# Gated attention into a routed expert layer on one core: fewer blocks in the DMA transposes, a z that is copied across, and a ring of row pairs

## The chip, the cores and the metric

One core of one Trainium2 chip. The metric is the device time of one execution in microseconds (us). TensorE (PE) multiplies, ScalarE (ACT) and VectorE (DVE) work element by element, GpSimd (POOL) issues the indirect transfers and all transfers that change the type, and SyncE (SP) issues the others; all transfers run on the same 16 DMA engines.

## The reference

```
B, S, D = 8, 2816, 256                      # u, v: (B, S, D) float32; z: (B, S, 64)
scores = z @ z.T / S                        # per batch
out    = u * (relu(scores)**2 @ v)
x      = out.reshape(22528, 256)
dense  = relu(x @ w1_dense) @ w2_dense      # 256 -> 512 -> 256
e, p   = argmax and softmax of x @ w_gate   # 8 experts
result = dense + p[e] * (relu(x @ w1[e]) @ w2[e])
```

## The kernel before

The program has two parts that meet in DRAM. The **attention part** goes through the 8 sequences (batches) in order. A sequence is 22 blocks of 128 tokens; blocks are numbered g = 0 to 175 over all sequences, and the program calls `tick(g)` once for each, about half-way and at the end of each pair of blocks; `at` and `soon` hang work on a tick by its number. The scores of a group of 2 or 4 query blocks against pairs of key blocks are made from zT, the transposed z, with two matmuls side by side on 64 rows of the array each (L408). For that, zT holds the 64 features of a block twice, on partitions 0 to 63 and 64 to 127. ScalarE and VectorE make relu and square (L423, L425, L436, L438) into a tile A. Since the scores are symmetric, part of A is not computed but transposed by DMA from an earlier group's A (L493), inside the tile of the later group or into the memory of the weights `wall`, which are loaded later. The product with v is L610, and it takes two finished blocks at a time.

`load_z` brings the next sequence's z in with GpSimd's queue. `turn_z`, called twice for a sequence at the border between two sequences, lets VectorE double 11 blocks of it (L115), and SP transposes the doubled copy, 11 blocks of 128 x 128 at a time (L118).

When two blocks are finished, `gate_x` multiplies them by u into `pays` (L637), a ring of 22 rows of 384 values, of which 256 are data, 4 hold the gate's value and the token's number and the rest is padding. SP transposes the pair for the router (L639): from the start of one row to the end of the data of the next, that is 5 blocks of 128 columns, of which 4 are data. `routing(q)` handles 11 blocks at once (fewer at the end, `sizes`), 5 ticks after the last of them: logits, the expert of each token, and its place in the list of its expert. `route_b` writes gate and token into the rows of `pays`, and `scatter(g)` casts the places of one block (L777) and has GpSimd write its 128 rows of 576 bytes to `xs` in DRAM (L779). One block is sent each tick (`one_scatter`, first come first served), two while rows 143 to 153 are waiting, each of these followed by a small copy on GpSimd (`paced`).

The **expert part** begins with rows 0 to 153, whose table of tiles (`table(0)`) is known by then; `fetch` (from tick 170 on, SP) reads 256 tokens of one expert transposed from `xs` (L954) with gates and tokens (L956). A `slot` is one such tile: `up` (L1003), relu on ScalarE (L1006), `down` for both experts (L1012), the sum (L1029, L1030), and the indirect write of the result by GpSimd (L1032), with a small copy (`pause`, L1017) behind the first half. The rows that are not yet sent go out between the slots: four at slot 0, two at slot 1, then one at each slot s with s % 6 == 4, each with a pause behind it. All must be gone before slot 61, from which on tiles need the second table. GpSimd's instructions run in the order in which the program gives them (`behind`).

The order of PE, ACT, DVE and SP is made while the program is built: `offer` hands out the work of ScalarE and VectorE by a model of the time (`now`, `free`), and each instruction waits in its engine's queue in that order.

Of the kernel before, what the change touches and what calls it, by code (L numbers as in the profile page):

```python
# [8 lines left out]
F32 = mybir.dt.float32  # L9
# [6 lines left out]
P = 128  # L16
# [3 lines left out]
def kernel(  # L20
# [34 lines left out]
    ROW = 288  # L55
    WIDE = 384
    CAP = N
# [43 lines left out]
    ecap = const.tile([P, E], F32, name="ecap")  # L101
    pays = const.tile([P, 2 * G, WIDE], BF, name="pays")

# [4 lines left out]

    def turn_z(b, k0, k1):

        if k0 == 0:
            assert not any(left[m] for m in left if groups[m][0] == b - 2)
            zn_of[b] = zpool.tile([P, nK, 2, dq], BF, name="zn", bufs=1)
            zT_of[b] = zpool.tile([P, nK, P], BF, name="zT")
# [7 lines left out]
        if k1 == nK:  # L122
            z_there.add(b)
# [17 lines left out]

    z_of, zn_of, zT_of, v_of, ut_of, xT_of, lg_of, rs = {}, {}, {}, {}, {}, {}, {}, {}

# [249 lines left out]
    def scores(n, ks, x=None):  # L393

        open_group(n)
        b, i0, w = groups[n]
        zT = zT_of[b]
        c = w * P
        while n == 0 and z0_left and parts0[z0_left[0]][0] <= ks[-1] + (4 if ks[0] else 1):
# [12 lines left out]
        relu(n, ks, s, c, now[0] + 0.2, sx)  # L412
        run(now[0] + (0.4 if n + ks[0] == 0 else 0.0))
# [59 lines left out]
    def block(n, k, c):  # L473

        w = groups[n][2]
        for a in far[n]:
            _, j0, wj = groups[a]
            if j0 <= k < j0 + wj:
                x = c * wj + k - j0
                return turned_to(a, n, w)[:, x * P:(x + 1) * P]  # L480
        return A[n][:, k, c * P:(c + 1) * P]

# [150 lines left out]
    def gate_x(g, o):  # L633
        g0 = g % (2 * G)
        x = pays[:, g0:g0 + 2, 0:D]
        assert g + 1 < 2 * G or (g - 2 * G in placed and g + 1 - 2 * G in placed)
        nc.vector.tensor_mul(x, o[:, :, 0:D], ut_of.pop(g))  # L637
        xT = aw.tile([P, 5, P], BF, name="xT", bufs=8)
        nc.sync.dma_start_transpose(  # L639
            out=xT[:], in_=pays[:, g0:g0 + 2, :].rearrange("p n r -> p (n r)")[:, 0:5 * P])  # L640
        issue(1.25)
        for j in range(2):
            xT_of[g + j] = xT[:, 3 * j:3 * j + 2, :]

# [62 lines left out]
    def route_b(q):  # L707
# [5 lines left out]
        def one():  # L713
            se = vec("se", n)
            nc.vector.tensor_reduce(out=se, in_=ex, axis=AX.X, op=ALU.add)
            o = starts[q] % (2 * G)
            rows = pays[:, o:o + n, :]
# [19 lines left out]
        def three():  # L737
            nc.vector.tensor_add(inc, inc, pre[1])
            nc.vector.tensor_mul(inc, inc, oh)
            pos = vec("pos", n, bufs=5)  # L740
            nc.vector.tensor_reduce(out=pos, in_=inc.rearrange("p e t -> p t e"),
                                    axis=AX.X, op=ALU.add)
            rs[q] = pos

# [23 lines left out]
    def paced(g):  # L768
        scatter(g)
        behind(lambda: nc.gpsimd.tensor_copy(rest[:], pays[:, g % (2 * G), 0:160]))  # L770

    def scatter(g):
        q = max(q for q in range(nQ) if starts[q] <= g)
        j = g - starts[q]

        pi = rt.tile([P, 1], I32, name="pi", bufs=16)
        nc.vector.tensor_copy(pi[:], rs[q][:, j:j + 1])  # L777
        free["pool"] = max(free["pool"], now[0]) + 1.5
        ins = behind(lambda: nc.gpsimd.indirect_dma_start(  # L779
            out=xs, out_offset=bass.IndirectOffsetOnAxis(ap=pi[:], axis=0),  # L780
            in_=pays[:, g % (2 * G), 0:ROW].bitcast(F32), in_offset=None))
        if q < Q1:
# [343 lines left out]
    placed = set()  # L1126

    def one_scatter(dve=True):
        if not waiting:
            return  # L1130
        g = waiting.pop(0)
        if dve:
            send = paced if (Q1 - 1) * G <= g < Q1 * G else scatter
            offer(now[0], 0, {"dve": (0.1, lambda eng: send(g))}, lambda t: placed.add(g))
        else:
            scatter(g)
            placed.add(g)

    routed = []
# [58 lines left out]
    def first_fetch(s):  # L1198
        assert not waiting or waiting[0] >= Q1 * G
        got[s] = fetch(s)  # L1200
# [7 lines left out]

    def tick(g):
        for fn in later.pop(g, []):  # L1210
            fn()
        one_scatter()
        if waiting and (Q1 - 1) * G <= waiting[0] < Q1 * G:
            one_scatter()
# [15 lines left out]
    late["y"] = pool("psY", 2, space=bass.MemoryType.PSUM)  # L1230
    for s in range(NT - MAYBE + 2):
        assert s + AHEAD < NT1 or not waiting, (s, len(waiting))
        slot(s, NT - MAYBE)
        for fn in later.pop(nB + s, []):
            fn()
        for _ in range(4 if s == 0 else 2 if s == 1 else s % 6 == 4):
            if waiting:
                g = waiting[0]
                one_scatter(dve=False)
                pause(pays[:, g % (2 * G), 0:ROW].bitcast(F32))  # L1240
    assert not waiting
# [39 lines left out]
```

## Time and profile before

| | us |
|---|---|
| median of 3 runs (905.73 to 906.49) | 906.41 |
| the profiled execution, its own time | 910.9 |
| its span, first to last instruction | 909.2 |
| TensorE busy in the span | 865.5 |
| VectorE, ScalarE, GpSimd busy | 669.7, 702.9, 486.0 |
| mean granted clock of TensorE | 0.992 of 2.4 GHz |

The rows below come from the one profiled execution, which took 4.5 us more than the median. Busy time of an engine that does not set the end says little; the views by stretch and the chain of waits tell which one does.

### The profile page before, as it was taken

What the parts mean: (1) busy time and instruction counts of PE and PEld (TensorE: products, weight loads), DVE (VectorE), ACT (ScalarE), POOL (GpSimd) and SP (SyncE); (2) the same over time, 40 slices, a digit from 0 to 9 for tenths busy, and PEclk for the clock granted to TensorE, in tenths of its full rate; (3) what the DMA queues carried; (4) which work ended last, traced back from release to release, by engine and by line L of the source; (5) the groups of instructions that cost most, each with busy time, mean ns of one, the idle gap of its engine ahead of it and who ended that gap; (6) DMA issues with size and microseconds to landing.
All of it is one profiled execution on the core that took longest, in us unless ns stands there. A gap on an engine that the chain in (4) does not pass through costs nothing.

```text
span 909.2 us, 30147 instructions
## 1 busy us (share of the span) xinstructions
PE 865.5 (95%) x12178; PEld 757.4 (83%) x12178; DVE 669.7 (74%) x1275; ACT 702.9 (77%) x873; POOL 486.0 (53%) x538
## 2 busy tenths in 40 slices
PE   7999897999999999999999999899999999999996
PEld 5898796898898898788898878688887888888885
DVE  8989695898997998897998985545654444546663
ACT  8989695897897897797897984566766776777664
POOL 7202343244344344344244374778787887777765
PEclk9999999999999999999999999999999999999999
DMA  8998999999999999999999867555544544544333
GB/s 175 174 199 152 179 175 133 172 196 199 194 190 174 200 177 163 192 204 180 200 170 179 148 143 135 118 123 113 113 113 108 115 111 115 112 102 102 92 94 86
DMA packets 289246, 136.80 MB, mean 150 GB/s; under 512 B 258638, under 2 KB 266062, under 8 KB 289104
## 3 DMA queue, kind: packets, MB, share of 16 engines
q1 hardware_dynamic: 263552, 79.40, 52.4%
q0 software_dynamic: 25552, 55.44, 27.4%
q8 instruction: 96, 1.57, 0.7%
q14 instruction: 46, 0.38, 0.1%
HBM read 61.54 MB, written 37.03 MB: 108 GB/s over the span
## 4 chain that ended last, share of the span: by engine, by line
PE 62%; POOL 15%; issue 12%; DVE 5%; DMA 3%; ACT 2%; POOLq 0%; another core or an unknown queue 0%; DVEq 0%; ACTq 0%
PE o L610 41%; POOL out_dram L1032 11%; PE s L408 9%; PE yy L1012 5%; PE h_ps L1003 5%; POOL zr L1017 3%; DMA wall<-A 1%; DVE r L425 1%; PE lg L671 1%; DMA vb<-in_v_dram 1%; ACT A L436 1%; DVE pays L637 1%; DVE ring L1030 1%; DVE A L438 1%; ACT r L423 1%
## 5 line engine op out<-in xcount | busy, mean ns | idle before, releaser
L610 PE MATMUL o<-vb,A 64*128 64x256 bf16 x7184 | 464.4, 270 | 8.5 <-issue 5.8
L610 PEld LDWEIGHTS <-A 64*128 64x128 bf16 x7184 | 381.5, 94 | 51.3 <-issue 10.7
L779 POOL DMA_INDIRECT xs<-pays,pi x176 | 189.1, 1075 | 281.2 <-DVE pi L777 232.5
L423 ACT ACTIVATE r<-s 128x1024 f32<-128x1024 f32 (+1 forms) x246 | 242.5, 1010 | 50.3 <-PE s L408 48.0
L436 ACT ACTIVATE A<-r 128x1024 bf16<-128x1024 f32 (+1 forms) x246 | 248.7, 1042 | 8.7 <-issue 3.1
L1006 ACT ACTIVATE ring<-h_ps 128x1024 bf16<-128x1024 f32 x180 | 184.6, 1026 | 90.8 <-PE h_ps L1003 51.7
L425 DVE TENSOR_SCALAR r<-s 128x1024 f32<-128x1024 f32 x151 | 182.8, 1219 | 14.3 <-PE s L408 12.4
L1030 DVE SCALAR_TENSOR_TENSOR ring<-yy,me,ring 128x256 f32<-128x256 f32 x179 | 86.3, 482 | 141.4 <-ACT ring L1029 70.9
L438 DVE TENSOR_TENSOR A<-r 128x1024 bf16<-128x1024 f32 x145 | 175.3, 1218 | 3.8 <-ACT r L423 2.8
L1032 POOL DMA_INDIRECT out_dram<-ring,me x140 | 145.5, 1039 | 54.9 <-DVE ring L1030 27.2
L1012 PEld LDWEIGHTS <-ring 128*128 128x128 bf16 x1432 | 139.3, 98 | 34.9 <-issue 17.1
L408 PE MATMUL s<-zT 64*128 64x512 bf16 (+1 forms) x874 | 146.9, 357 | 7.7 <-ACT r L423 2.4
L1012 PE MATMUL yy<-w2d,ring 128*128 128x256 bf16 x716 | 107.8, 273 | 12.2 <-DVE ring L1030 11.6
L1012 PE MATMUL yy<-ring 128*128 128x256 bf16 x716 | 107.9, 273 | 2.4 <-ACT ring L1006 1.4
L1003 PE MATMUL h_ps<-ring,w1d 128*128 128x256 bf16 x720 | 93.7, 274 | 2.6 <-ACT ring L1006 2.6
L1003 PE MATMUL h_ps<-ring 128*128 128x256 bf16 (+1 forms) x872 | 93.5, 253 | 0.6 <-ACT ring L1006 0.6
L990 DVE COPY ring<-wall 128x2048 bf16 x109 | 82.9, 775 | 11.6 <-issue 7.1
L637 DVE TENSOR_TENSOR pays<-o,ut 128x512 bf16<-128x512 f32 x88 | 60.2, 684 | 38.7 <-PE o L610 16.9
L1029 ACT COPY ring<-yy 128x256 f32<-128x256 f32 x179 | 67.3, 376 | 23.2 <-PE yy L1012 11.4
L1003 PEld LDWEIGHTS <-ring 128*128 128x128 bf16 x872 | 73.5, 98 | 8.5 <-issue 1.2
L1003 PEld LDWEIGHTS <-w1d 128*128 128x128 bf16 x720 | 70.2, 98 | 11.2 <-issue 2.9
L408 PEld LDWEIGHTS <-zT 64*128 64x128 bf16 x874 | 54.7, 94 | 23.9 <-issue 11.2
(124 smaller groups left out, 448.2 us busy)
## 6 DMA issues: line engine op xcount, KB each, us to landing
ut<-in_u_dram SPq DMA_DIRECT2D x88, 256.0 KB
vb<-in_v_dram POOLq DMA_DIRECT2D x14, 704.0 KB
wall<-in_moe_w_dram POOLq DMA_DIRECT2D x16, 256.0 KB
xs<-pays,pi POOLq DMA_INDIRECT x176
zr<-in_z_dram POOLq DMA_DIRECT2D x7, 352.0 KB
out_dram<-ring,me POOLq DMA_INDIRECT x140
ring<-xs SPq DMA_TRANSPOSE x114
xT<-pays SPq DMA_TRANSPOSE x88
```

Of the source, the lines that this page charges most:

```text
L408: nc.tensor.matmul(out=s[:, h, y * c:(y + 1) * c], lhsT=zT[r, k + h, :], rhs=zT[r, i0:i0 + w, :], start=True, stop=True)
L423: nc.scalar.activation(r[:, :, :c], s[:, :, :c], AF.Relu, scale=1.0 / S)
L425: nc.vector.tensor_scalar(out=r[:, :, :c], in0=s[:, :, :c], scalar1=1.0 / S, scalar2=0.0, op0=ALU.mult, op1=ALU.max)
L436: nc.scalar.activation(a, r, AF.Square)
L438: (nc.gpsimd if eng == "pool" else nc.vector).tensor_mul(a, r, r)
L610: nc.tensor.matmul(out=o[:, j, 0:D], lhsT=block(n, k, i + j - i0)[r], rhs=v_of[b][r, k, :], start=(p == 0 and x == 0), stop=(p == 1 and x ...
L779: ins = behind(lambda: nc.gpsimd.indirect_dma_start(out=xs, out_offset=bass.IndirectOffsetOnAxis(ap=pi[:], axis=0), in_=pays[:, g % (2 * G ...
L1003: nc.tensor.matmul(out=h_ps[:, f, hs, :], lhsT=w1(c, f), rhs=xT[:, hs, c, :], start=(c == 0), stop=(c == 1))
L1006: nc.scalar.activation(h[:, :, 0:m * P], h_ps[:, :, 0:m, :].rearrange("p f h t -> p f (h t)"), AF.Relu)
L1012: nc.tensor.matmul(out=y[:, k, :], lhsT=h[:, f, j * P:(j + 1) * P], rhs=w2(f), start=(f == 0), stop=(f == 3))
L1030: nc.vector.scalar_tensor_tensor(out=ys, in0=y[:, 1, :], scalar=me[:, j, 0:1], in1=yd, op0=ALU.mult, op1=ALU.add)
L1032: ins = behind(lambda: nc.gpsimd.indirect_dma_start(out=out, out_offset=bass.IndirectOffsetOnAxis(ap=ids[j], axis=0), in_=ys, in_offset=No ...
```

## The change

The transposed part of a finished pair is now exactly its data: `pays` holds 16 pairs of 544 values, in which the second row's data follow the first row's at once, so 4 blocks are transposed instead of 5. The first row's gate and token now lie on the first 4 values of the second row; so these are written only when the row is sent (L777's place; the cast of the places is made once for each routing), and the first row of a pair may go only 4 ticks after the second (3 for rows 143 to 153). `next_row` picks the next one: a first row whose partner left long enough ago, else a second row. z is transposed as it is loaded, two blocks of 64 features in one of 128 columns, so in 11 blocks and one transfer; every second column block of zT is filled. VectorE then copies the two halves across the partitions (`cross_z`), at ticks 9 and 11 of the sequence before. Where the halves of a block pair now stand in the other order, the indices of A follow (`block`). Late rows go out at every fifth slot.

```diff
+    WIDE = 2 * D + ROW - D
+    PAIRS = 16
+    pays = const.tile([P, PAIRS, WIDE], BF, name="pays")
+    def row(g):
+        return pays[:, g // 2 % PAIRS, g % 2 * D:g % 2 * D + ROW]
-    def turn_z(b, k0, k1):
-        nc.vector.tensor_copy(
-            zn_of[b][:, k0:k1, :, :],
-            z_of[b][:, k0:k1, :].unsqueeze(2).to_broadcast([P, k1 - k0, 2, dq]))
+    def turn_z(b):
+        assert not any(left[m] for m in left if groups[m][0] == b - 2)
+        zT_of[b] = zpool.tile([P, nK, P], BF, name="zT")
         nc.sync.dma_start_transpose(
-            out=zT_of[b][:, k0:k1, :],
-            in_=zn_of[b][:, k0:k1].rearrange("p k h d -> p (k h d)"))
+            out=zT_of[b].rearrange("p (j e) c -> p j e c", e=2)[:, :, 0, :],
+            in_=z_of[b][:].rearrange("p k d -> p (k d)"))
+    def cross_z(b, h):
+        zT = zT_of[b].rearrange("p (j e) c -> p j e c", e=2)
+        r, o = (slice(x * dq, (x + 1) * dq) for x in (h, 1 - h))
+        nc.vector.tensor_copy(zT[r, :, 1, :], zT[o, :, 0, :])
+        if h == 1:
             z_there.add(b)
...
-    nc.vector.memset(pays[:, :, D:], 0.0)
+    nc.vector.memset(pays[:, :5, :], 0.0)
+    nc.vector.memset(pays[:, 5:, 2 * D:], 0.0)
...
-                nc.tensor.matmul(out=s[:, h, y * c:(y + 1) * c], lhsT=zT[r, k + h, :],
+                nc.tensor.matmul(out=s[:, h, y * c:(y + 1) * c], lhsT=zT[r, k + h * own, :],
...
-        xT = aw.tile([P, 5, P], BF, name="xT", bufs=8)
-        nc.sync.dma_start_transpose(
-            out=xT[:], in_=pays[:, g0:g0 + 2, :].rearrange("p n r -> p (n r)")[:, 0:5 * P])
+        xT = aw.tile([P, 4, P], BF, name="xT", bufs=8)
+        nc.sync.dma_start_transpose(out=xT[:], in_=x)
...
-            nc.vector.reciprocal(rows.bitcast(F32)[:, :, P], se)
-            nc.vector.tensor_copy(rows.bitcast(I32)[:, :, P + 1], tok[:, starts[q]:starts[q + 1]])
+            gt = gt_of[q] = rt.tile([P, G, 2], F32, name="gt", bufs=5)
+            nc.vector.reciprocal(gt[:, :n, 0], se)
+            nc.vector.tensor_copy(gt[:, :n, 1].bitcast(I32), tok[:, starts[q]:starts[q + 1]])
...
+            pi = rt.tile([P, G], I32, name="pi", bufs=5)
+            nc.vector.tensor_copy(pi[:, :n], pos)
...
-        pi = rt.tile([P, 1], I32, name="pi", bufs=16)
-        nc.vector.tensor_copy(pi[:], rs[q][:, j:j + 1])
+        nc.vector.tensor_copy(row(g)[:, D:D + 4].bitcast(F32), gt_of[q][:, j, :])
...
-            soon(t - 1 if b else 5, lambda b=b: turn_z(b + 1, 0, nK // 2), 0.4)
-            soon(t if b else 6, lambda b=b: turn_z(b + 1, nK // 2, nK), 0.4)
+            at(t - 1 if b else 5, lambda b=b: turn_z(b + 1))
+            for h in range(2):
+                soon(t + 9 + 2 * h, lambda b=b, h=h: cross_z(b + 1, h), 0.8)
...
+    def next_row():
+        even = [g for g in waiting if g % 2 == 0 and
+                sent.get(g + 1, 9e9) <= clock[0] - (3 if (Q1 - 1) * G <= g < Q1 * G else 4)]
+        odd = [g for g in waiting if g % 2]
+        return (even or odd or [None])[0]
...
-        for _ in range(4 if s == 0 else 2 if s == 1 else s % 6 == 4):
+        for _ in range(4 if s == 0 else 2 if s == 1 else s % 5 == 4):
```

## Rows read from the trace of the kernel before

**Rows 1.** The page of the profile, its parts 1 and 2: busy time of the engines over the whole execution; then the 40 slices of the span, of TensorE and the DMA engines, in tenths.

```profile
...
PE 865.5 (95%) x12178; PEld 757.4 (83%) x12178; DVE 669.7 (74%) x1275; ACT 702.9 (77%) x873; POOL 486.0 (53%) x538
...
PE   7999897999999999999999999899999999999996
...
DMA  8998999999999999999999867555544544544333
...
```

**Rows 2.** The page, its part 3: the queue of SP (packets, megabytes, share of the 16 engines' span), and the view of DMA issues: the two transposes that the change touches.

```profile
...
q1 hardware_dynamic: 263552, 79.40, 52.4%
...
xT<-pays SPq DMA_TRANSPOSE x88
...
zT<-zn SPq DMA_TRANSPOSE x14
...
```

**Rows 3.** Busy time of each engine by stretch of 5 us, with the granted clock, the share of the 16 DMA engines and the rate, before and in two halts of TensorE.

```profile
...
75.00:80.00 5.00, 5.00 (x87) 4.54 (x85) 4.92 (x9) 5.00 (x6) 2.75 (x3) 1.00 0.43 92
...
85.00:90.00 5.00, 5.00 (x90) 4.73 (x88) 5.00 (x7) 5.00 (x6) 1.94 (x2) 1.00 1.16 199
...
95.00:100.00 5.00, 4.91 (x94) 4.15 (x90) 1.73 (x7) 1.53 (x3) 1.94 (x2) 1.00 1.10 201
...
105.00:110.00 5.00, 4.73 (x48) 3.05 (x49) 3.37 (x12) 3.94 (x5) 0.97 (x1) 0.66 1.06 222
145.00:150.00 5.00, 4.52 (x77) 4.03 (x73) 4.97 (x10) 4.76 (x6) 2.77 (x4) 1.00 1.01 61
150.00:155.00 5.00, 0.84 (x10) 0.68 (x12) 0.97 (x2) 0.56 (x1) 1.72 (x2) 0.94 1.16 186
...
```

**Rows 4.** The chain of work that ended last, 80 to 112 us (start, length, what).

```profile
...
95.45 7.64 DMA wall<-A
...
103.25 1.06 ACT A L436
...
```

**Rows 5.** Who waited for whom, 90 to 110 us (us in total, times, longest).

```profile
...
ACT A L436 <- DMA wall<-A: 3.0, 1, 3.0
...
PE s L408 <- ACT r L423: 2.4, 1, 2.4
...
```

**Rows 6.** What SP's queue issued, 76 to 104 us (start, time that the issue took).

```profile
...
83.25 1.81 SPq L639 DMA_TRANSPOSE xT<-pays  x1
...
86.50 3.72 SPq L118 DMA_TRANSPOSE zT<-zn  x2
...
91.46 2.25 SPq L493 DMA_TRANSPOSE wall<-A  x1
94.14 1.21 SPq L639 DMA_TRANSPOSE xT<-pays  x1
95.45 2.22 SPq L493 DMA_TRANSPOSE wall<-A  x1
...
```

**Rows 7.** Who waited for whom on SP's queue, the whole span: the z transposes.

```profile
...
SPq L118 <- DVE pi L777: 8.5, 6, 2.2
...
SPq L118 <- DVE A L438: 5.1, 2, 4.7
...
```

**Rows 8.** Groups of instructions by line and shape: VectorE's copies and casts near the change.

```profile
...
L425 DVE TENSOR_SCALAR r<-s 128x1024 f32<-128x1024 f32 x150 | 182.2, 1222 | 14.3 <-PE s L408 12.4 <-ACT A L436 1.2
...
L990 DVE COPY ring<-wall 128x2048 bf16 x109 | 82.9, 775 | 11.6 <-issue 7.1 <-DVE ring L1030 2.9
...
L777 DVE CAST pi<-pos 128x1 int32<-128x1 f32 x176 | 25.5, 155 | 0.1
...
L115 DVE COPY zn<-zr 128x1408 bf16<-128x1408 bf16 x14 | 12.2, 872 | 0.0
...
```

**Rows 9.** What GpSimd did from 564.67 us on, by group: the row scatters and what is put behind each.

```profile
...
L779 POOL DMA_INDIRECT xs<-pays,pi x17 | 17.5, 1027 | 6.7 <-DVE pi L777 3.5 <-issue 3.2
L1017 POOL COPY zr<-pays 128x144 f32<-128x144 f32 x16 | 5.5, 341 | 0.0
```

**Rows 10.** GpSimd's timeline around one late scatter.

```profile
...
590.74 0.98 POOL L779 DMA_INDIRECT xs<-pays,pi  x1 [0.17 <-issue]
591.71 0.32 POOL L1017 COPY zr<-pays 128x144 f32<-128x144 f32 x1
...
```

**Rows 11.** Who waited for whom, 585 to 800 us, in which ten of the late scatters lie.

```profile
...
POOL out_dram L1032 <- DVE ring L1030: 20.1, 21, 1.9
...
PE yy L1012 <- DVE ring L1030: 8.2, 10, 1.6
...
```

**Rows 12.** The row scatters over the whole span: how many, durations in ns, first and last start.

```profile
...
L779 POOL DMA_INDIRECT xs<-pays,pi x176: 960/974/1728, 73.7 to 789.6; - x176
...
```

**Rows 13.** The chain over the whole span: two transfers of GpSimd's queue that something waited for, from the start of the span and from the expert part.

```profile
...
5.16 8.21 DMA vb<-in_v_dram
...
669.09 2.27 DMA out_dram<-ring,me
...
```

**Rows 14.** GpSimd's timeline at the end of the rows that the first table needs, and what SP and TensorE do next in theirs.

```profile
...
544.79 0.98 POOL L779 DMA_INDIRECT xs<-pays,pi  x1 [1.15 <-DVE pi L777]
...
553.58 0.93 SPq L954 DMA_TRANSPOSE ring<-xs  x1
...
564.67 1.05 PE L1003 MATMUL h_ps<-ring,w1d 128*128 128x256 bf16 x8
...
```

**Rows 15.** TensorE's timeline at its longest halt.

```profile
...
154.16 1.50 PE L610 MATMUL o<-vb,A 64*128 64x256 bf16 x13 [4.64 <-issue]
...
```

More of the change, by code (lines that the diff above doesn't have):

```diff
@@ L55 @@
     ROW = 288
-    WIDE = 384
+    WIDE = 2 * D + ROW - D
     CAP = N
@@ L101 @@
     ecap = const.tile([P, E], F32, name="ecap")
-    pays = const.tile([P, 2 * G, WIDE], BF, name="pays")
+    PAIRS = 16
+    pays = const.tile([P, PAIRS, WIDE], BF, name="pays")
+    def row(g):
+        return pays[:, g // 2 % PAIRS, g % 2 * D:g % 2 * D + ROW]
     def load_z(b):
@@ L140 @@
     z_there = {0}
-    z_of, zn_of, zT_of, v_of, ut_of, xT_of, lg_of, rs = {}, {}, {}, {}, {}, {}, {}, {}
+    z_of, zn_of, zT_of, v_of, ut_of, xT_of, lg_of, rs, gt_of = {}, {}, {}, {}, {}, {}, {}, {}, {}
     sync = [10.0]
@@ L398, in scores @@
         c = w * P
+        own = b == 0
         while n == 0 and z0_left and parts0[z0_left[0]][0] <= ks[-1] + (4 if ks[0] else 1):
@@ L473, in block @@
     def block(n, k, c):
-        w = groups[n][2]
+        b, _, w = groups[n]
         for a in far[n]:
@@ L478, in block @@
             if j0 <= k < j0 + wj:
-                x = c * wj + k - j0
+                x = c * wj + (k - j0 ^ (c & 1 if b else 0))
                 return turned_to(a, n, w)[:, x * P:(x + 1) * P]
+        c ^= k & 1 if b else 0
         return A[n][:, k, c * P:(c + 1) * P]
@@ L633, in gate_x @@
     def gate_x(g, o):
[L634 to L637, printed above, removed]
-        xT = aw.tile([P, 5, P], BF, name="xT", bufs=8)
-        nc.sync.dma_start_transpose(
-            out=xT[:], in_=pays[:, g0:g0 + 2, :].rearrange("p n r -> p (n r)")[:, 0:5 * P])
+        x = pays[:, g // 2 % PAIRS, 0:2 * D]
+        assert all(x < 0 or x in placed for x in (g - 2 * PAIRS, g + 1 - 2 * PAIRS))
+        nc.vector.tensor_mul(x.rearrange("p (n d) -> p n d", n=2), o[:, :, 0:D], ut_of.pop(g))
+        xT = aw.tile([P, 4, P], BF, name="xT", bufs=8)
+        nc.sync.dma_start_transpose(out=xT[:], in_=x)
         issue(1.25)
         for j in range(2):
-            xT_of[g + j] = xT[:, 3 * j:3 * j + 2, :]
+            xT_of[g + j] = xT[:, 2 * j:2 * j + 2, :]
     def vec(name, a, b=1, dt=F32, **kw):
@@ L769, in paced @@
         scatter(g)
-        behind(lambda: nc.gpsimd.tensor_copy(rest[:], pays[:, g % (2 * G), 0:160]))
+        behind(lambda: nc.gpsimd.tensor_copy(rest[:], row(g)[:, 0:160]))
     def scatter(g):
@@ L774, in scatter @@
         j = g - starts[q]
-        pi = rt.tile([P, 1], I32, name="pi", bufs=16)
-        nc.vector.tensor_copy(pi[:], rs[q][:, j:j + 1])
+        nc.vector.tensor_copy(row(g)[:, D:D + 4].bitcast(F32), gt_of[q][:, j, :])
         free["pool"] = max(free["pool"], now[0]) + 1.5
         ins = behind(lambda: nc.gpsimd.indirect_dma_start(
-            out=xs, out_offset=bass.IndirectOffsetOnAxis(ap=pi[:], axis=0),
-            in_=pays[:, g % (2 * G), 0:ROW].bitcast(F32), in_offset=None))
+            out=xs, out_offset=bass.IndirectOffsetOnAxis(ap=rs[q][:, j:j + 1], axis=0),
+            in_=row(g).bitcast(F32), in_offset=None))
         if q < Q1:
@@ L1126 @@
     placed = set()
-    def one_scatter(dve=True):
-        if not waiting:
-            return
-        g = waiting.pop(0)
+    sent = {}
+    clock = [0]
+    def next_row():
[3 more added lines that the diff above has]
+        return (even or odd or [None])[0]
+    def one_scatter(dve=True):
+        g = next_row()
+        if g is None:
+            return None
+        waiting.remove(g)
+        sent[g] = clock[0]
         if dve:
@@ L1137, in one_scatter @@
             placed.add(g)
+        return g
     routed = []
@@ L1198, in first_fetch @@
     def first_fetch(s):
-        assert not waiting or waiting[0] >= Q1 * G
+        assert min(waiting, default=nB) >= Q1 * G
         got[s] = fetch(s)
@@ L1209, in tick @@
     def tick(g):
+        clock[0] = g
         for fn in later.pop(g, []):
@@ L1212, in tick @@
         one_scatter()
-        if waiting and (Q1 - 1) * G <= waiting[0] < Q1 * G:
+        if any((Q1 - 1) * G <= g < Q1 * G for g in waiting):
             one_scatter()
@@ L1231 @@
     for s in range(NT - MAYBE + 2):
+        clock[0] = nB + s
         assert s + AHEAD < NT1 or not waiting, (s, len(waiting))
@@ L1235 @@
             fn()
-        for _ in range(4 if s == 0 else 2 if s == 1 else s % 6 == 4):
[L1237 to L1240, printed above, removed]
+        for _ in range(4 if s == 0 else 2 if s == 1 else s % 5 == 4):
+            g = one_scatter(dve=False)
+            if g is not None:
+                pause(row(g).bitcast(F32))
     assert not waiting
```

11 lines of the change are left out of this document (2 added, 9 removed).

## The prediction

> **What bounds the kernel now.** I read the page from the top. TensorE is busy 95% of the span [rows 1], so there is little to win where it is busy; what a change of transfers can win lies in its halts. The slices under it show where to look: in the first 24 of 40, the attention part, the DMA engines stand at eight or nine tenths and more, and in the expert part at three to five [rows 1]. So two things are full in the attention part, and the question is whether the fuller DMA ever stops TensorE. The view by stretch answers it: TensorE is busy 5.00 of 5.00 us in nearly all stretches, and two are far from that. One is 150 to 155 us with 0.84; the other lies between 100 and 110 us [rows 3].
>
> The halt near 103 us is the one that this change can reach. The waits name it: ScalarE waits 3.0 us for a transpose of A (it may not overwrite an A that is still being read), and TensorE waits 2.4 us for ScalarE [rows 5]. The chain gives the transfer: issued at 95.45, landed 7.64 us later [rows 4]. After it the granted clock of TensorE is 0.66 over 5 us [rows 3], a part of them at 1.2 instead of 2.4 GHz; that costs (1 - 0.66) x 5 = 1.7 us more. So this halt is worth 2.4 + 1.7 = 4.1 us. Why the transfer is slow stands in SP's queue: from 83 us on it puts out a pair's 5 blocks, a transpose of A, both z transposes together (the issue alone 3.72 us), two more of A, and another pair [rows 6]; and the DMA share goes from 0.43 at 75 us to over 1 [rows 3] (packets overlap, so it passes 1).
>
> The halt at 149.5 us is 4.64 us long and no wait explains it [rows 15]; while the DMA share is 1.01, only 61 GB/s move [rows 3]. With a low clock behind it like the first one's 1.7 us it costs about 6 us. The profiled execution took 910.9 us, 4.5 more than the median, so I take this halt to be mostly its own, and the sum below, made against 910.9, is carried over to 906.4 without it.
>
> In the expert part GpSimd is close behind TensorE: it is kept from its next write only 20.1 us in 215, and TensorE waits 8.2 us in ten pieces for sums that wait for GpSimd's ring [rows 11]. Ten late scatters lie in this stretch, so one piece each: 0.8 us for a late scatter.
>
> **The change, part by part.**
>
> Fewer blocks. A block is 128 x 128 values of 2 bytes, 32.8 KB. Of the pairs' transposes, 88 [rows 2] go from 5 blocks to 4: 88 blocks less. Of z's, 14 transposes of 11 become 7: 77 less. What a block costs, estimated from SP's queue: 52.4% of 909.2 us for 79.40 MB [rows 2] is 6.0 us a MB, so 0.20 us of all 16 engines. 165 blocks are 33 us of DMA time in some 560. TensorE is not waiting for it except at the halt. There, one of the two z transposes (11 blocks) and a block each of two pairs are gone from the queue ahead of the late transfer: 13 blocks. At 0.20 us that is 2.6 us; at the pace of the late transfer itself, 16 blocks by the code in 7.64 us, or 0.48 a block, it is 6.2. The nearer row is the queue's mean, so 2.6 of the 3.0 us that ScalarE waited; 0.4 us are left, and TensorE, which waited 0.6 less than ScalarE did, does not halt. Bounds: minus 4.1 us with the clock; nothing, if the halt stays as it is. I take minus 4.1.
>
> The skill's page "DMA: Bandwidth & Descriptors" (section "Latency and other measured facts") speaks against part of this: the Trainium skill gives DMA transposes about 30% less rate where the middle dimension isn't contiguous, and z's target now skips every second block. No row here has such a target. By it the 11 blocks of the new z transpose would cost like 14 and 10 instead of 13 would be saved, 2.0 us by the queue's mean; ScalarE would wait 1.0, TensorE some 0.4 with no fall of the clock, and the sum would be 0.4 us worse.
>
> SP's issues. Seven z transposes fewer, and the one left no longer waits on VectorE; the two largest such waits were 8.5 and 5.1 us over the span [rows 7]. What stands behind in the queue, u and A's transposes, comes earlier. A zero in the sum, since no halt but the one above is put down to them.
>
> VectorE. 14 copies at 872 ns go [rows 8], and 14 of 1,408 values on 64 partitions come, across partitions, which no row shows. Between the rate of the weight copy (775 ns for 2,048, so 0.53 us) and that of the float scale from PSUM (1,222 ns for 1,024, so 1.68 us) [rows 8]: minus 4.8 to plus 11.3 us of VectorE's time. A copy within bf16 is nearest to the old one, so zero. The per-row cast (155 ns) becomes a copy of two values of about that length, and a cast for each of 18 routings comes: 18 x 0.155 = 2.8 us over the span. VectorE has 239 us free, and ScalarE shares its work by the planner; nothing on the path. The copies are queued at ticks 9 and 11 of a sequence, and the scores of the next can be begun at tick 14 at the earliest, when its first group is two ahead of the one in hand; the transpose they read was put out ten ticks, 31 us, before. The larger memset at the start is two in place of one for about as many words, a few tenths of a us at most, next to loads that are still coming; zero.
>
> The new wait. Before VectorE writes a first row's gate, the scatter of the second row must have been read out; on VectorE's queue all relu and squares stand behind. The scatters go out 159 times between 73.7 and 564.7 us [rows 9, 12], so a tick is 3.1 us and 4 ticks are 12.4. The landing of a scatter isn't shown; a write of GpSimd's queue in the quiet part took 2.27 us, and a load among others at the start 8.21 [rows 13]. Both are below 12.4, also with a scatter's own 1 us on GpSimd. So zero; if the cover is gone, a stall of 3 us on that side cost 4.1 us above.
>
> The late rows. Going through `next_row` with one row a tick, and each routing's rows there 4 ticks after they are due (which gives the 16 of [rows 9] by the old rule), 17 rows are left at the end of the attention part: a tick passes empty when the last first row of a routing has its partner in the next. One more late scatter with its pause takes 0.98 + 0.32 us and two gaps of 0.17 on GpSimd [rows 10], 1.6 us. The price on the path is between 0 and that; by the ten pieces, 0.8. Every fifth slot instead of the sixth is 1.6 / 18 more of GpSimd's time for 1.6 / 22, some 1.5%, inside its 9% of waiting.
>
> The first fetch. The last of rows 0 to 153 leaves GpSimd at 544.79, SP fetches at 553.58 and TensorE starts on it at 564.67 [rows 14]. A first row now goes 3 ticks (9.3 us) behind its partner, so about 554; landed at 556.4 by the 2.27 us of [rows 13], while TensorE needs the fetched tile 8 us later. Zero.
>
> Sum: 910.9 - 4.1 + 0.8 = 907.6 for an execution like the profiled one; 906.4 - 3.3 = **903.1 us** for the median.
>
> **The rivals.** One: the halt isn't in the timed runs, or another transfer of that crowded stretch is late instead, as each order of the planner is a new one. Then only the late scatter counts, 906.4 + 0.8 = 907.2, or with the clock's part alone won, 905.5. For it: only one execution is profiled, and the halt's place depends on 3 us. Against it: the order is fixed, and the same queue meets the same border each time.
>
> Two, the other side: the wait on the second row. It decides if scatters land later than 12.4 us after their tick, as they can when a load of v stands before them in GpSimd's queue; two such stalls on VectorE at 4.1 us give 906.4 + 0.8 + 8.2 = 915, one beside a halt that is gone 907, one beside one that stays 911. Against it: 8.21 us for the load among others.
>
> Three: GpSimd becomes the bound of the slots. It decides if the late rows are two or more above 16 and each costs its full 1.6 us: 906.4 + 3.2 = 909.6 without the gain. Its ring of sums then shows more waits than ten.
>
> Four: the first fetch comes late, from the point where the last row lands after about 560 us: some 3 us, 909.
>
> **How the numbers follow.** The halt gone: 0.49, 899.5 to 904.6, where the low end takes what the freer queues may give in other places. Rival one: 0.29, 904.6 to 908.2. Two 0.10, three 0.07, four 0.05. A measurement of this kernel can tell about 0.2%, 1.8 us. So faster 0.49, same 0.29, slower 0.22. The range leaves one in ten on each side: 899.5 to 909.5; the likeliest case alone reaches from 899.5 to 904.6.
>
> **What would show it.** In the profile after: no wait of ScalarE for A's transposes near 100 us and a clock of 1.00 there; queue q1 with some 5.4 MB less; 17 late scatters and about 11 waits of TensorE for the sums between the first and the last of them; no wait of VectorE's small gate copies for a scatter. Wrong it would be if the halt stands, if VectorE waits for transfers to `xs`, or if the expert part grew by over 2 us.

## The result and the profile after

The changed kernel takes 916.25 us (median of 6 runs, 913.52 to 919.01), the kernel before 906.17 us (6 runs, 905.73 to 907.09): the ratio on record is 1.0086, interval 1.0059 to 1.0113, and that of the two medians 1.0111. It is slower; 903.1 was forecast. The profiled execution took 916.6 us, its span 914.5.

The halt near 103 us that the forecast rested on is gone. The waits of the kernel after, 90 to 110 us, hold no ScalarE that waits for a transpose of A [rows 5], and the stretches of 5 us that answer to [rows 3] (stretch, length, busy PE, PEld, DVE, ACT, POOL, granted clock, DMA share, GB/s) show a full clock:

```profile
ACT r L430 <- PE s L415: 0.4, 1, 0.4
PE s L415 <- DVE r L432: 0.5, 1, 0.5
```

```profile
100.00:105.00 5.00, 4.47 (x75) 3.51 (x71) 4.86 (x11) 4.86 (x5) 0.00 (x0) 1.00 0.99 170
105.00:110.00 5.00, 5.00 (x87) 4.52 (x85) 4.86 (x10) 4.78 (x6) 0.97 (x1) 1.00 0.87 182
```

In its place stands one of 0.5 us, TensorE waiting for VectorE's relu; it will matter. SP's queue moves 5.40 MB less, as forecast, and the 16 late scatters of [rows 9] are 16 again, not 17:

```profile
q1 hardware_dynamic: 242208, 74.00, 45.1%
```

```profile
L785 POOL DMA_INDIRECT xs<-pays,pi x16 | 16.7, 1046 | 5.1 <-DVE pays L783 2.6 <-issue 2.3 <-DVE se L721 0.2
```

Most of the loss is in the expert part. Stretches of 50 us, the kernel before first, then after; columns as above:

```profile
600.00:650.00 50.00, 48.12 (x440) 42.78 (x439) 29.34 (x63) 35.40 (x55) 39.61 (x46) 1.00 0.52 116
650.00:700.00 50.00, 48.50 (x441) 42.75 (x439) 28.29 (x61) 34.10 (x54) 39.44 (x46) 1.00 0.47 114
```

```profile
600.00:650.00 50.00, 46.32 (x415) 40.17 (x413) 27.84 (x60) 32.05 (x50) 38.53 (x45) 1.00 0.50 108
650.00:700.00 50.00, 44.34 (x399) 38.70 (x397) 24.09 (x56) 32.95 (x52) 34.81 (x42) 1.00 0.41 103
```

GpSimd is no busier there (34.81 of 50 against 39.44) and the late rows are 16, so the condition of rival three isn't met. The waits from 585 to 800 us, against [rows 11]: TensorE waits 13.6 us for sums where it waited 8.2, and ScalarE 25.6 for TensorE where it waited 18.2 (the kernel before first, then after).

```profile
ACT ring L1006 <- PE yy L1012: 18.2, 13, 1.8
```

```profile
POOL out_dram L1038 <- DVE ring L1036: 26.8, 22, 2.5
ACT ring L1012 <- PE yy L1018: 25.6, 16, 3.3
PE yy L1018 <- DVE ring L1036: 13.6, 13, 1.6
```

How such a halt comes about, in the timeline of the kernel after (start, length, engine, what, in brackets the idle time before it and what ended it):

```profile
654.60 1.04 PE L1009 MATMUL h_ps<-ring 128*128 128x256 bf16 x8
655.67 1.02 ACT L1012 ACTIVATE ring<-h_ps 128x1024 bf16<-128x1024 f32 x1 [0.46 <-PE h_ps L1009]
656.35 1.04 PE L1009 MATMUL h_ps<-ring,w1d 128*128 128x256 bf16 x8
660.23 1.02 ACT L1012 ACTIVATE ring<-h_ps 128x1024 bf16<-128x1024 f32 x1 [3.27 <-PE yy L1018]
661.61 0.48 DVE L1036 SCALAR_TENSOR_TENSOR ring<-yy,me,ring 128x256 f32<-128x256 f32 x1 [3.71 <-issue]
662.14 0.60 PE L1018 MATMUL yy<-w2d,ring 128*128 128x256 bf16 x4 [1.27 <-DVE ring L1036]
```

The matmuls that the second relu reads end at 657.39; the relu before it started 0.03 us after its own matmuls had ended (655.64), this one starts 2.84 us after. The matmul that the view names as its releaser comes later in TensorE's order than the one it needs. The trace also holds the times at which TensorE's semaphore counted up (the count by which it signals finished work, and the only one that this relu waits for): after 656.53 the next are 660.21, 660.30, 660.40 and 660.49, as many as there are groups of matmuls that had ended since, at 657.39, 658.26, 659.14 and 660.00. So the work was done, by the ends that the view gives, and the signals came late and together; VectorE's sum, TensorE and GpSimd follow.

### The profile page after: what moved, and what is told of

It is laid out like the page before. It is cut to its first block, busy times and chain, and to the rows that moved or that the text cites. A ratio compares the mean times of both kernels' runs of the same rounds, so it can differ in the third digit from the quotient of the medians.

```text
span 914.5 us, 30087 instructions
## 1 busy us (share of the span) xinstructions
PE 867.0 (95%) x12178; PEld 758.1 (83%) x12178; DVE 673.5 (74%) x1296; ACT 700.0 (77%) x871; POOL 495.8 (54%) x538
## 3 DMA queue, kind: packets, MB, share of 16 engines
q1 hardware_dynamic: 242208, 74.00, 45.1%
## 4 chain that ended last, share of the span: by engine, by line
PE 80%; issue 6%; POOL 4%; DMA 4%; DVE 3%; ACT 2%; another core or an unknown queue 0%; POOLq 0%; DVEq 0%; ACTq 0%
PE o L618 42%; PE yy L1018 14%; PE h_ps L1009 13%; PE s L415 9%; POOL out_dram L1038 3%; DMA xs<-pays,pi 2%; DMA vb<-in_v_dram 1%; PE lg L677 1%; DVE ring L1036 1%; DVE r L432 1%; POOL zr L1023 1%; ACT ring L1035 1%; ACT r L430 1%; ACT ring L1012 0%; ACT A L443 0%
## 5 line engine op out<-in xcount | busy, mean ns | idle before, releaser
L785 POOL DMA_INDIRECT xs<-pays,pi x176 | 202.7, 1152 | 270.9 <-DVE pays L783 225.6
L430 ACT ACTIVATE r<-s 128x1024 f32<-128x1024 f32 x248 | 244.1, 1011 | 41.2 <-PE s L415 39.1
L443 ACT ACTIVATE A<-r 128x1024 bf16<-128x1024 f32 (+1 forms) x242 | 245.3, 1045 | 3.9 <-issue 2.4
L432 DVE TENSOR_SCALAR r<-s 128x1024 f32<-128x1024 f32 x149 | 180.0, 1221 | 10.4 <-PE s L415 7.4
L445 DVE TENSOR_TENSOR A<-r 128x1024 bf16<-128x1024 f32 x149 | 179.4, 1216 | 1.3 <-ACT r L430 0.7
L1009 PE MATMUL h_ps<-ring 128*128 128x256 bf16 (+1 forms) x872 | 95.7, 256 | 0.9 <-ACT ring L1012 0.5
L996 DVE COPY ring<-wall 128x2048 bf16 x109 | 82.6, 772 | 11.5 <-issue 6.5
```

The lines of the kernel that those rows point to most:

```text
L430: nc.scalar.activation(r[:, :, :c], s[:, :, :c], AF.Relu, scale=1.0 / S)
L432: nc.vector.tensor_scalar(out=r[:, :, :c], in0=s[:, :, :c], scalar1=1.0 / S, scalar2=0.0, op0=ALU.mult, op1=ALU.max)
L443: nc.scalar.activation(a, r, AF.Square)
L445: (nc.gpsimd if eng == "pool" else nc.vector).tensor_mul(a, r, r)
L785: ins = behind(lambda: nc.gpsimd.indirect_dma_start(out=xs, out_offset=bass.IndirectOffsetOnAxis(ap=rs[q][:, j:j + 1], axis=0), in_=row(g) ...
L1009: nc.tensor.matmul(out=h_ps[:, f, hs, :], lhsT=w1(c, f), rhs=xT[:, hs, c, :], start=(c == 0), stop=(c == 1))
```

## The experiments

The chip of experiments 1 to 4 runs the kernel before in 872 us, the others in 900 to 906, so each ratio is against the kernel before on the same chip. All kernels compute the whole reference. "z part" are the lines of `turn_z`, `cross_z`, `own` and `block`, "ring part" all the rest of the diff.

| | kernel | median us | ratio to before, interval |
|---|---|---|---|
| 1 | before, every fifth slot | 874.09 | 1.0023 (0.9978 to 1.0068) |
| 2 | after, every sixth slot | 872.81 | 1.0005 (0.997 to 1.0039) |
| 3 | z part alone | 871.88 | 0.9979 (0.9928 to 1.003) |
| 4 | ring part alone | 880.16 | 1.0089 (1.0051 to 1.0127) |
| 5 | after | 904.76 | 1.0045 (1.0019 to 1.0072) |
| 6 | after, rows early, three a tick | 912.89 | 1.013 (1.0085 to 1.0175) |
| 7 | after, every sixth slot | 905.12 | 1.0058 (1.0022 to 1.0095) |
| 8 | both edits of 6 and 7 | 910.2 | 1.0121 (1.008 to 1.0163) |
| 9 | z part alone | 905.8 | 1.005 (1.0016 to 1.0084) |
| 10 | ring part alone | 910.68 | 1.0087 (1.0058 to 1.0116) |
| 11 | after, rows early, two a tick | 910.65 | 1.0088 (1.0056 to 1.012) |
| 12 | after | 907.18 | 1.0036 (1.001 to 1.0063) |
| 13 | before | 899.5 | 0.999 (0.9962 to 1.0018) |
| 14 | before, loads of v a tick later | 902.74 | 1.001 (0.9973 to 1.0047) |
| 15 | before, late rows a slot earlier | 901.19 | 0.9995 (0.9963 to 1.0028) |
| 16 | z part alone, loads of v a tick later | 908.23 | 1.0068 (1.0032 to 1.0105) |
| 17 | ring part alone, every sixth slot | 907.2 | 1.0063 (1.003 to 1.0096) |
| 18 | ring part alone | 908.56 | 1.0069 (1.0024 to 1.0113) |

Each trace holds 12,178 matmuls in nearly the same order, so the traces can be cut at equal ones. The time in us between the starts of two of them, by their number, worked out from the records (in the kernel before, 1500 to 2000 holds the halt near 103 us, 2500 to 8480 the rest of the attention part to 524 us, 9200 to 9270 the first expert tiles; 2000 to 2500, with the halt at 149.5 us that only the first profile has, is left out):

| profile | 1500-2000 | 2500-8480 | 8480-9200 | 9200-9270 | 9270-12177 |
|---|---|---|---|---|---|
| before, first profile | 34.2 | 354.6 | 46.8 | 13.1 | 318.5 |
| 13, before | 32.1 | 351.4 | 47.4 | 15.2 | 314.0 |
| 14, before, v later | 29.9 | 354.8 | 50.7 | 14.5 | 314.1 |
| 15, before, late rows | 34.1 | 355.2 | 47.1 | 14.4 | 316.9 |
| 9, z part | 30.5 | 358.4 | 49.9 | 12.5 | 317.9 |
| 10, ring part | 33.8 | 356.9 | 49.1 | 11.5 | 325.5 |
| 17, ring part, sixth slot | 32.6 | 354.6 | 48.9 | 11.4 | 323.0 |
| after, first profile | 30.5 | 356.9 | 50.2 | 13.5 | 328.4 |
| 5, after | 30.3 | 357.6 | 51.1 | 11.7 | 320.8 |
| 12, after | 30.3 | 357.1 | 50.4 | 8.9 | 325.1 |
| 7, after, sixth slot | 30.3 | 358.5 | 50.8 | 13.1 | 317.3 |
| chip of 1 to 4: 1, before, fifth slot | 34.1 | 349.2 | 45.2 | 6.8 | 300.3 |
| 3, z part | 29.4 | 349.2 | 45.3 | 6.8 | 300.3 |
| 4, ring part | 31.4 | 355.4 | 45.8 | 11.4 | 300.3 |
| 2, after, sixth slot | 29.4 | 349.9 | 45.5 | 10.2 | 300.3 |

**1 to 4, parts and spacing.** One and two turn one line each way; three and four are the change with the lines of the other part taken back. Four also has its first fetch at `nB - 5 + s`, one tick later than both the kernel before and the kernel after (`nB - 6 + s`); so have 6, 8, 10, 11, 17 and 18. Where the expectations of 6 and 10 call this the tick of the kernel before, they are mistaken.

```diff
-        for _ in range(4 if s == 0 else 2 if s == 1 else s % 6 == 4):
+        for _ in range(4 if s == 0 else 2 if s == 1 else s % 5 == 4):
```

> The kernel before with one number changed: late rows leave at every fifth slot instead of every sixth (the 16 late rows stay 16, the last leaves at slot 49 instead of 58). Theory one (the closer late rows cost the expert part: GpSimd has no room to catch up between them): slower than before by 5 to 10 us, 911 to 916, with the halts of TensorE for the sums between 590 and 765 us up from 8 us to 13 or more. Rival (what is lost comes from the ring of pairs or from z, and the spacing costs nothing): 905 to 908, the halts stay at about 8 us in all.

> The changed kernel with every sixth slot restored; all else of the change stays. Theory one: 906 to 911, the halts of the expert part back near 8 us. Rival: no gain, 914 to 919, with halts of the same size at other places.

> The kernel before with the z part of the change alone: one transpose of 11 blocks a sequence, the copies across, the indices of A. Pairs, scatters and late rows are as before. If the free DMA queue helps as the first 500 us of the changed kernel look: 898 to 904. If the other order that the planner makes costs what it gives: 904 to 908. If the z part is the cause of the loss: 910 or more.

> The ring of pairs alone: 4 blocks transposed for a pair, the first row 4 ticks later, every fifth slot; z is doubled and transposed in two halves as before. In this order the last of rows 0 to 153 leaves a tick later, so the five first fetches of the expert part are one tick later as well. If the loss sits in the ring with its late rows: 912 to 919. If it sits in z: 903 to 908.

On this chip the ring part costs 0.9%, and z alone and the whole with the sixth slot can't be told from no change (the whole with the fifth slot wasn't run on it). The fifth slot is not the cost: from 9270 on all four take 300.3 us, and TensorE is never without work (3, the z part alone):

```profile
600.00:650.00 50.00, 50.00 (x460) 44.76 (x459) 30.70 (x68) 37.13 (x58) 42.44 (x52) 1.00 0.59 126
650.00:700.00 50.00, 50.00 (x460) 44.76 (x459) 24.89 (x46) 36.67 (x58) 41.34 (x50) 1.00 0.53 120
```

What the ring costs in both kernels that have it lies between 9200 and 9270: 10.2 and 11.4 us instead of 6.8. Four loses 6.2 us more between 2500 and 8480 (355.4 against 349.2), with a halt of 3.04 us at 284.7 and a granted clock of 0.66 behind it; 18 has a halt of 5.24 us at the same instruction, 10 and 17 have none there, and its cause wasn't found. SP's queue in 2 (first the wait, 530 to 557 us; then the timeline):

```profile
SPq L960 <- DMA xs<-pays,pi: 2.6, 1, 2.6
```

```profile
549.70 1.21 SPq L960 DMA_TRANSPOSE ring<-xs  x1
551.63 2.26 SPq L646 DMA_TRANSPOSE xT<-pays  x1
554.38 1.20 SPq L960 DMA_TRANSPOSE ring<-xs  x1
556.31 1.52 SPq L646 DMA_TRANSPOSE xT<-pays  x1
559.53 0.26 PE L677 MATMUL lg<-wg,xT 128*128 128x8 bf16 x4 [3.20 <-DMA xT<-pays]
```

and in 3, without the ring:

```profile
548.00 1.24 SPq L642 DMA_TRANSPOSE xT<-pays  x1
553.19 0.34 PE L674 MATMUL lg<-wg,xT 128*128 128x8 bf16 x8
```

SP waits for the last row's scatter before its first fetch; the last transposed pair, whose gating VectorE has ended at 548.77, stands behind the fetches and is put out at 556.31, and TensorE, which is there at 556.3, waits 3.20 us. Without the ring it is put out 2.1 us after its gating and there long before. By the order in the code row 152 leaves one tick before the first fetch, where row 153 left three before it in the kernel before (the expectation of 5 says four).

**5 to 8, the entry and the spacing where the kernel before takes 901 us.** Six has these lines, eight the sixth slot too:

```diff
-        return (even or odd or [None])[0]
+        first = [g for g in odd if (Q1 - 1) * G <= g < Q1 * G]
+        return (first or even or odd or [None])[0]
...
-        at(nB - 6 + s, lambda s=s: first_fetch(s))
+        at(nB - 5 + s, lambda s=s: first_fetch(s))
...
-        if any((Q1 - 1) * G <= g < Q1 * G for g in waiting):
-            one_scatter()
+        for _ in range(2):
+            if any((Q1 - 1) * G <= g < Q1 * G for g in waiting):
+                one_scatter()
```

> The changed kernel itself, beside the kernel before on one chip. Theory E (entry): the ring sends the last row that the first fetch needs one tick before that fetch, where the kernel before leaves four ticks; SyncE then waits 2.6 to 4.3 us for the scatter, the last transpose of a finished pair stands behind it, and TensorE halts some 3.2 us for it at the first late logits, with a lower clock behind it: +3.4 to +4.6 us between TensorE's instructions 9200 and 9270; the halt near 103 us is gone (-2 to -4.7 us). By it the time stands within 3 us of the kernel before on a chip whose expert part runs without halts (slots every 1.74 us), and the rest of the loss on the first chip lies in that part alone. Rival S (spacing): a late row every fifth slot costs some 8 to 10 us wherever it runs: about 0.9 to 1.1% over the kernel before on this chip too.

> The changed kernel, but rows 143 to 153 send their odd row first and may send three in a tick, and the first fetches stand one tick later as in the kernel before: the last of these rows leaves five ticks ahead of the first fetch. Theory E: SyncE's wait for the scatter and TensorE's wait of 3 us for the last transposed pair are gone, and the time is 3.4 to 4.6 us under the changed kernel on the same chip. Rival S: no difference from the changed kernel, within 1.5 us.

> The changed kernel with a late row every sixth slot, as in the kernel before. Theory E: within 1.5 us of the changed kernel where the expert part runs without halts; TensorE's wait for the last pair is still there. Rival S: 8 us under the changed kernel.

> Both edits: rows 143 to 153 early, and a late row every sixth slot. Theory E: as the kernel with the early rows alone, 3.4 to 4.6 us under the changed kernel and 1 to 4 us under the kernel before. Rival S: 8 us under the changed kernel, as the sixth slot alone.

The fifth slot as a cause falls (904.76 with it, 905.12 without), and so does the hope for the early rows: 8 us worse, and 5 us with the sixth slot. In 6, with three rows a tick, VectorE reaches a first row's gate before the second row has been read, the wait of rival two, and TensorE, busy 45.28 of 50 us in short pieces, falls to a lower clock (waits from 515 to 560 us, then the stretch):

```profile
DVE pays L783 <- DMA xs<-pays,pi: 2.7, 1, 2.7
```

```profile
500.00:550.00 50.00, 45.28 (x671) 34.44 (x668) 40.23 (x90) 37.85 (x43) 30.68 (x35) 0.90 0.75 131
```

From 8480 to 9200 it takes 55.0 us, and 55.7 in 8, against 51.1 in 5. But 8 has no such wait in its whole trace, and the same mean clock (first 8, then 11, the early rows with two a tick):

```profile
500.00:550.00 50.00, 43.08 (x657) 33.55 (x653) 38.68 (x99) 35.55 (x39) 28.30 (x34) 0.90 0.61 121
```

```profile
500.00:550.00 50.00, 45.10 (x712) 37.38 (x708) 40.51 (x103) 37.48 (x41) 31.10 (x36) 0.93 0.73 133
```

The clock is at its lower level for 10.2 us in 6 and 8, 6.8 in 11, 3.4 in 5 and not at all in 12. So the lower clock is most of what the early rows lose there; that the wait of rival two brings it about isn't shown.

**9 to 12, the parts on such a chip.** 9 is the kernel of 3, 10 that of 4; 11 is 6 without its third piece.

> The kernel before with the z part alone (11 blocks a sequence, copied across late), beside the other part on one chip. Theory T (two parts of opposite sign): the halt near 103 us is gone and the ring's wait at the first late logits isn't there: 2 to 5 us under the kernel before. Rival U (no gain anywhere): the halt near 103 us isn't in most timed runs, so within 1.5 us of the kernel before.

> The ring part alone (4 blocks transposed for two rows, 16 shared pairs, the even row four ticks later, a late row every fifth slot), first fetches on the tick of the kernel before. Theory T: 5 to 9 us over the kernel before, the halt near 103 us still there and TensorE waiting some 3 us for the last transposed pair. Rival U: as the changed kernel, 4 us over the kernel before.

> The changed kernel with rows 143 to 153 led by their odd rows, two in a tick as before, and the first fetches one tick later: the last of these rows leaves three ticks ahead of the first fetch and not one, and no even row comes closer than five ticks behind its odd row. If the entry wait is what the ring costs: SyncE's wait for the scatter under 1 us, TensorE's for the last pair gone, 3 us under the changed kernel. If the slower time with three rows in a tick came from these rows' order and not from VectorE's wait for a scatter: 4 to 8 us over the changed kernel, as there.

> The changed kernel itself once more, the measure for the three others. Theory T: 2 to 8 us over the kernel before on a chip whose kernel before takes some 900 us, within 3 us of it on one where it takes some 870 us; the z part and the ring part add up to it within 3 us.

z alone is slower here, though its halt near 103 us is gone (30.5 against 32.1 to 34.2), and the parts don't add up (0.5% and 0.9%, together 0.4%). Part of what z wins it loses again: TensorE halts 0.45 to 0.52 us at the same instruction of six sequences (1520, 2657, 3794, 4931, 6068, 7205), where the kernels without the z part have none in any profile, nor have 2 and 3 on their chip. The timeline there in 9:

```profile
368.08 0.71 PE L674 MATMUL lg<-wg,xT 128*128 128x8 bf16 x22
369.61 0.25 DVE L684 TENSOR_REDUCE m<-lg 128x11 f32<-128x88 f32 x1 [2.36 <-PE s L410]
370.91 2.57 DVE L427 TENSOR_SCALAR r<-s 128x1024 f32<-128x1024 f32 x2
372.40 0.39 PE L410 MATMUL s<-zT 64*128 64x512 bf16 x2 [0.46 <-DVE r L427]
```

and in 3, the same kernel on the other chip:

```profile
361.24 0.71 PE L674 MATMUL lg<-wg,xT 128*128 128x8 bf16 x22
361.98 0.25 DVE L684 TENSOR_REDUCE m<-lg 128x11 f32<-128x88 f32 x1 [1.58 <-PE lg L674]
```

There VectorE starts 0.03 us after the logits end (361.95), here 0.82 us after (368.79); the routing's steps shift, the relu behind them too, and TensorE, which has a few tenths to spare at this point of z's order, waits. All nine profiles with the z part on these chips bear this out: TensorE halts 0.45 to 0.59 us at one of these six instructions wherever VectorE starts 0.81 us or more after the logits (35 times), and under 0.1 us where it starts within 0.43 (19 times). The kernels without the z part have signals up to 1.43 us late and no halt there.

With the early rows two a tick (11) TensorE's wait for the last pair is gone, and the time is 3.5 us worse than that of 12: 8480 to 9200 takes 52.5 us against 50.4. The entry decides nothing on this chip, since TensorE waits between 9200 and 9270 in every kernel (7.7 to 15.2 us for what takes 6.8).

**13 to 16, is it any shift?**

```diff
-                soon(t + (13, 15)[h], lambda b=b, h=h: load_v(b + 1, h, 2))
+                soon(t + (14, 16)[h], lambda b=b, h=h: load_v(b + 1, h, 2))
```

That is 14, and 16 on the z part; 15 has `s % 6 == 3` for `s % 6 == 4`.

> The kernel before, unchanged, run as if it were a changed one: the zero of the comparison, and a second profile of it. Theory N (no stage of its own: on the chips whose kernel before takes some 900 us, signals between TensorE and ScalarE come 1 to 4 us late now and then, and every shift of the work moves which of them hurt): ratio 1 within 0.2%; the halt near 103 us is in its profile, the one at 149 us isn't. Theory P (each part has its own price): the same.

> The kernel before with the two loads of v one tick later: nothing added, nothing taken away. Theory N: 0.2 to 0.8% over the kernel before, as the z part alone was. Theory P: within 0.2% of it.

> The kernel before with its late rows one slot earlier in each group of six. Theory N: 0.2 to 0.8% over the kernel before, out of the expert part. Theory P: within 0.2% of it.

> The z part alone, with the same later loads of v. Theory N: anywhere from 0.4% under to 0.8% over the kernel before, and not as the z part alone by more than 0.2%. Theory P: as the z part alone, 0.5% over the kernel before, within 0.2%.

Two neutral edits cost nothing that can be measured (0.10 and minus 0.05%, intervals up to 0.47 and 0.28%), z alone 0.5% and with the later loads of v 0.7%. So my theory that any shift costs finds no support, and z has a price of its own here. The halt at 149 us is not in 13, as the prediction took it, and after the halt near 103 us its clock does not fall, where it does in the first profile and in 15:

```profile
PE s L408 <- ACT r L423: 2.2, 1, 2.2
```

```profile
105.00:110.00 5.00, 3.41 (x54) 2.56 (x55) 3.19 (x12) 5.00 (x6) 0.97 (x1) 1.00 0.94 189
```

And in 14 the halt is gone (29.9 us), with no block fewer: so it also depends on when v is loaded.

**17 and 18, the ring part's 0.9%.** 17 has the sixth slot and the `first` lines of 6 (without them one row is left over).

> The ring part alone with a late row every sixth slot again; rows 143 to 153 lead with their odd rows, without which one row would be left over, the last of them still two ticks ahead of the first fetch. If the fifth slot costs what the profiles of six kernels with it and eight without it show between TensorE's instructions 9270 and the end (323.5 us against 317.3): 4 to 7 us under the ring part alone, so 1 to 4 us over the kernel before. If their timed runs tell more (904.76 with it, 905.12 without): as the ring part alone within 2 us.

> The ring part alone once more, on the same chip: 0.7 to 1.0% over the kernel before by either.

907.2 and 908.56: again no price of the spacing that these runs can tell. From 9270 on, ten profiles with the ring part on these chips take 316.8 to 328.4 us, mean 322.6; the six without it 314.0 to 318.9, mean 316.7 (322.4 and 315.7 without those of 16, 18 and the first of the kernel before, whose executions took 4.5 to 11.3 us more than the medians). On the chip of 1 to 4 it is 300.3 in all. So the ring loses some 6 us in the expert part where signals come late, and nothing where they don't. It isn't shown that it meets more of them: of the 180 relus there 39 to 48 start over 0.3 us after both the matmul they need and ScalarE's instruction before, against 37 to 47 without the ring (means 43 and 41; none on the chip of 1 to 4). But TensorE's halts come to 16.0 us in the mean with the ring and 11.7 without. Why the same lateness costs more stays open. Rows of their own with four ticks of lag, which would part the order from the shared columns, weren't run.

## Why the prediction was wrong, step by step

- **The halt, minus 4.1.** It went, as forecast, but the size was that of one execution. Of the 4.1 us, 1.7 were a fall of the clock that 13 doesn't show. Between 1500 and 2000 the kernels before take 34.2, 32.1 and 34.1 us, those after 30.5, 30.3 and 30.3: 3.1 us in the mean. It goes with the z part (29.4 in 3, 30.5 in 9) and stays with the ring part (31.4, 33.8 and 32.6 us in 4, 10 and 17). How much of this is fewer blocks isn't shown, since the step "SP's issues", put at zero, moved too. z's transpose now leaves at 78.55 us, where the last of the two left after 86.50, and the second transpose of A into `wall` at 90.96, where the late one left at 95.45 [rows 6] (SP's queue of the kernel after):

```profile
78.55 1.79 SPq L117 DMA_TRANSPOSE zT<-zr  x1
90.96 3.24 SPq L501 DMA_TRANSPOSE wall<-A  x1
```

  14 shows that rival one's doubt about its place was fair.
- **VectorE and the planner, zero: wrong.** The copies cost what the lower bound said (the view of groups after, 60 to 130 us):

```profile
L126 DVE COPY zT<-zT 64x1408 bf16<-64x1408 bf16 x2 | 1.1, 554 | 0.1
```

  What I left out is where the planner puts the other work once they have moved. "ScalarE shares its work by the planner; nothing on the path" was true of the sum of busy time and not of the order: halts of half a microsecond at the six instructions, all six in 9 (2.9 us), three, four and five of them in the three profiles of after (1.6, 2.0 and 2.6 us). From 2500 to 8480 these three profiles take 3.5 us more than those of before, 13 and 15 (357.2 against 353.7); 2.0 us of this are TensorE's halts (4.1 against 2.1), the rest isn't put down to anything.
- **Around the tables, nothing said.** 8480 to 9200 takes 50.6 instead of 47.1 in the same profiles. Single late signals stand there (2.0 us in 5 and 12, 3.8 in 9), but 14 has one of 4.4 too, so this price is less sure.
- **The new wait, zero: nothing speaks against it.** The first profile of after has two such waits, 2.1 us together over the span, 5 and 12 have none. What it costs when the cover goes stays open: 6 has three, 6.9 us together, but 8 loses as much there with none.
- **The late rows, plus 0.8.** 16 are left, not 17. TensorE waits for sums 13 times, not 11, but with as many late rows; in 5 it is 9 times, and on the chip of 1 to 4, with as many late rows, TensorE has no halt there at all. So the ten pieces, from which the price of a late scatter was taken, weren't the scatters'. For the fifth slot the zero holds as far as the runs can tell (5 against 7, 17 against 18).
- **The first fetch, zero: wrong, as rival four.** I set the landing of the last row against TensorE's need of the fetched tile, 8 us later, and didn't ask what stands behind the waiting fetch in SP's queue: the last pair's transpose, which TensorE needs sooner. It costs 3.4 to 4.6 us on the chip where the rest has no halts (of the 4.6, 1.7 are a lower clock). On the chip of the result it isn't to be seen: 9200 to 9270 takes 13.5 us against 13.1.
- **The expert part, plus 0.8: wrong, and the largest piece.** The late row was the only term there, and the ring of pairs had none. It takes 324.8 instead of 316.5 us in the same six profiles, 8.3 us, far over the 2 us that the prediction itself had named as a sign of being wrong. Of these, 5.6 us are halts of TensorE (17.3 against 11.7) and 2.0 a lower clock. By 9, 10 and 17 it is the ring's; its cause stays open beyond the late signals.
- **The page on DMA.** SP's transfers took 45.1% of 914.5 us for 74.00 MB, 5.6 us a MB, against 6.0 before: the loss that the Trainium skill's page "DMA: Bandwidth & Descriptors" (section "Latency and other measured facts") gives for a middle dimension that isn't contiguous doesn't show in the queue's sum. The seven z transposes are only some 2.5 MB of it, so this settles little.

The pieces of after against before on these chips: minus 3.1, plus 3.5, plus 3.5, minus 2.9 (9200 to 9270, 11.4 against 14.2), plus 8.3, and minus 0.6 before 1500, together some 9 us; 2000 to 2500, left out for the halt at 149.5 us, would take off 2.4. Without the first profile of the kernel before they come to 9.5 us, with the same signs. The timed ratios of three chips give 0.4 to 0.9%, 3 to 8 us; the medians of the first alone lie 10.1 us apart.

## What to carry to other kernels

A halt that is taken away is won only if the order that replaces it has slack at the next border; look there for the engine with a few tenths to spare, not at its busy time. A wait that a transfer's queue takes over is priced by what stands behind it in that queue. A halt seen in one profile is a term of the sum only in so far as a second profile of the same kernel has it too, and a neutral edit does not remove it.

## What the runs showed of the hardware

At about the same granted clock (0.994 to 0.998 over the span on the one, 0.988 to 0.997 on the others) one chip ran the expert part in 300.3 us and the others in 314 to 328, with nearly the same durations of the single instructions (from 600 to 850 us, matmuls of 256 columns 273 ns in 3 and 273 to 275 in 9, relus 1,023 and 1,031). The difference is in signals from TensorE: from the end of the logits to VectorE's start 0.04 to 0.13 us in the first thirteen routings of 1, 2 and 3 (in 4 two take 0.66 and 0.45), and 0.4 to 1.4 us in three to six of the same thirteen on the other chips; in the expert part there, a relu starts at the worst 2.0 to 3.2 us after both its matmul's end and ScalarE's instruction before. The Trainium skill's page "Perfetto Trace Analysis" (section "Tensor Engine Instruction (MATMUL, LD_WEIGHTS)") says that a matmul's end in the profile is computed, and that its signal is pushed only when PSUM has acknowledged the data: the late step would lie behind the end that these rows show. The traces agree in so far as the matmuls behind go on, and the four semaphore updates within 0.28 us at 660.21 (result) come up to 2.8 us after the ends that they tell of; none shows what holds them back. I found no transfer and no fetch of instructions that goes with the late signals, and what makes them late is not known.
